# Eight softmax weight transposes on the DMA queue instead of TensorE, under a new order of the pieces

## The chip, the core and the metric

The kernel runs on one core of a Trainium2 chip. The metric is the device time of one execution in microseconds (us). Shorthand: PE is TensorE, DVE is VectorE, ACT is ScalarE, POOL is GpSimd, SP is SyncE, which here only issues transfers. SBUF is the on-chip working memory, PSUM the memory that PE writes its products to. Each engine takes its own instructions strictly in order and waits on semaphores.

## The reference

A cross attention between 512 tokens `x` and 32 state vectors `state`, for 8 batches and 8 heads of width 64, feeds a two-layer network with squared ReLU:

```python
scores  = scale * x @ state.T                    # 512 x 32
a       = softmax(scores, over the states)       # "rows"
xread   = a @ state
scores2 = scale * state @ x.T                    # 32 x 512
a2      = softmax(scores2, over the tokens)      # "columns"
sread   = a2 @ x
h = concat([xread, sread]) @ w_in                # 4352 x 512 by 512 x 2048
r = maximum(h, 0)
out = (s * r * r + b) @ w_out                    # 4352 x 2048 by 2048 x 512
```

The token rows of `xread` and the state rows of `sread` all go through the same two layers.

## The kernel before

**Pieces.** The work is cut into some 740 pieces, each a small Python function that issues a few instructions. `ORDER` (line 15) is a list of strings; the loop at line 735 walks through it and calls the pieces one after the other. A word is a name and its arguments, with the engine as a letter (A is ACT, V is DVE, G is POOL): `s.2.4.2.G` squares blocks 4 and 5 of batch 2 on POOL. There is no scheduler behind it (`manual_schedule`, line 132): the order of the words is the order on every engine and on every issuing queue. Semaphore waits between engines follow from the data and from the buffers.

**One batch b of tokens.** POOL issues the loads, which cast to 16 bits (`x`, line 182; `xn`, the same tokens in another layout, line 193). DVE transposes blocks of 32 (`xT`), PE makes the scores (`T`, line 304), DVE turns them (`U`, line 326) and takes maximum, difference (`D`, on DVE or POOL), sum and quotient (`z`, `At`) around ACT's exponential (`E1`); `A` is the row softmax. `keep` (line 320) has ACT copy the same PSUM scores to SBUF for later. PE multiplies the states into `w_in` (`M`, line 437), and ACT or DVE copies the product out (`Mc`). Then come 16 pieces `l` of layer 1 (two matmuls of 512 columns each), whose ReLU always runs on ACT (line 476), and the squares `s` on ACT, DVE or POOL (line 484). The buffers of the ReLU results turn among three, and layer 1 has two PSUM buffers. Batch 0 does a part of this in halves (`lh`, `sh`).

**Layer 2.** Batches 0 and 1 use plain products (`L`, line 512, four matmuls each). Batches 2 to 7 and the state rows use a fast 2 by 2 block multiplication with seven products (`P`, line 597, eight matmuls of 256 columns each) into PSUM tiles X, Y and W. It needs sums of blocks of the squares (`S`, line 576) and of `w_out` (`wsum`), and DVE evictions (`ev`, line 611) between products of one tile. `put` (line 619) and `out` issue the stores from SP.

**The column softmax, where the change is.** `E2` (line 388) is ACT's exponential with sums; `a2` (line 395) on DVE divides, giving 128 partitions by 1024 elements of 16 bits. `aps` (line 405) transposes this by eight PE matmuls with the identity, of 128 by 128 each, into a PSUM tile. `a2T` (line 411) copies the tile to SBUF, on ACT for seven batches and on DVE for one. `V` (line 414) is the product with `xn`, `srd` (line 434) its copy on ACT into `srdT`. All eight batches must have passed here before layer 1 of the state rows (`lsr`, line 507), near the end.

Of the kernel before, what the change touches and what calls it, by code (L numbers as in the profile page):

```python
# [11 lines left out]
FP16 = mybir.dt.float16  # L12
# [70 lines left out]
def kernel(  # L83
# [12 lines left out]
    nc = tc.nc  # L96
# [307 lines left out]

    def at_aps(b):
        at[b]["aps"] = aps = blocks(two_banks(f"aps_{b}", FP16), 0)
        for g in range(NG):
            for c in range(SCH):
                transp(aps[:, SCH * g + c], at[b]["a2"][:, g, P * c : P * c + P])

    def at_a2T(b, e):
        copy(e, sm(b, "a2T", [P, NG * SCH, P], FP16, apool, 2), at[b]["aps"])

    def at_V(*bs):

        pair = two_banks(f"vps_{bs[0]}")
# [87 lines left out]
    def square_half(b, f, p, e):  # L504
        squared(e, new_G(b, S)[:, f : f + 2, HALF * p : HALF * p + HALF], R_t.pop((b, f, p)))

    def layer1_sr(f):
        layer1("sr", f, [(w_in_f(k, f), srdT[:, k].rearrange("p n b -> p (n b)")) for k in range(NK)], B * Ns)

    ops_t = {}  # L510

    def layer2(tag, rr, q):
        if q == 0:
            ops_t[tag, rr] = ps_o.tile([P, DM], FP32, name=f"ops_{tag}_{rr}", tag="po")
        for f in range(4 * q, 4 * q + 4):
            nc.tensor.matmul(  # L516
# [252 lines left out]
```

## Time and profile before

| | |
|---|---|
| three runs | 217.42, 217.94, 218.0 us; median 217.94 |
| profiled execution | span 215.7 us from the first to the last instruction; the profile gives no other time of it, so 2.2 us of the median lie around the span |
| busy | PE 205.8 us, DVE 179.6, ACT 158.0, POOL 86.9 |
| mean granted PE clock | 0.992 |
| the eight `a2T` copies | ACT 7 of 1015 ns, DVE 1 of 681 ns |

The page gives busy time and share per engine, then the span in 40 slices of 5.4 us in which each digit is a tenth of busy time, then the DMA queues, the chain of work that ended last, and the costliest groups of instructions. A group's line gives the source line, the engine, what is written and read with its shape, the count, busy time and mean duration, and how long the engine had been idle just before such instructions and for whom. Back-to-back instructions overlap a little in the records, so mean times count is more than busy time.

### The profile page before, as it was taken

What the parts mean: (1) busy time and instruction counts of PE and PEld (TensorE: products, weight loads), DVE (VectorE), ACT (ScalarE), POOL (GpSimd) and SP (SyncE); (2) the same over time, 40 slices, a digit from 0 to 9 for tenths busy, and PEclk for the clock granted to TensorE, in tenths of its full rate; (3) what the DMA queues carried; (4) which work ended last, traced back from release to release, by engine and by line L of the source; (5) the groups of instructions that cost most, each with busy time, mean ns of one, the idle gap of its engine ahead of it and who ended that gap; (6) DMA issues with size and microseconds to landing.
All of it is one profiled execution on the core that took longest, in us unless ns stands there. A gap on an engine that the chain in (4) does not pass through costs nothing.

```text
span 215.7 us, 4829 instructions
## 1 busy us (share of the span) xinstructions
PE 205.8 (95%) x1955; PEld 130.0 (60%) x1955; DVE 179.6 (83%) x277; ACT 158.0 (73%) x260; POOL 86.9 (40%) x94
## 2 busy tenths in 40 slices
PE   7489999999999999999999999999999999999992
PEld 2134343344444448767677677677766777888881
DVE  2997899999998799969998999999986874593661
ACT  4598886899899788799999887779768475734300
POOL 8554126445093033157437057007223308916400
PEclk9969999999999999999999999999999999999999
DMA  6999998127849719523900939608902600440045
GB/s 153 175 207 206 196 206 146 41 63 106 137 106 140 133 20 171 68 50 64 162 24 2 187 112 115 82 17 145 221 8 46 144 11 0 102 97 0 5 147 145
DMA packets 23658, 22.43 MB, mean 104 GB/s; under 512 B 4436, under 2 KB 17492, under 8 KB 23636
## 3 DMA queue, kind: packets, MB, share of 16 engines
q0 software_dynamic: 16848, 12.52, 41.3%
q1 hardware_dynamic: 5504, 8.66, 14.9%
q10 hardware_dynamic: 1284, 0.95, 1.7%
q8 instruction: 15, 0.25, 0.5%
q14 instruction: 7, 0.06, 0.1%
HBM read 25.72 MB, written 8.91 MB: 161 GB/s over the span
## 4 chain that ended last, share of the span: by engine, by line
PE 91%; DMA 3%; ACT 2%; POOL 1%; DVE 1%; issue 0%; POOLq 0%
PE hps L472 25%; PE opf_X L141 20%; PE ops L516 13%; PE opf_W L141 10%; PE opf_Y L141 5%; PE mps L141 5%; DMA w_in<-in_moe_w_in_dram 3%; PE hps_sr L472 3%; PE vps L141 2%; PE aps L141 2%; PE ops_sr_X L141 2%; PE T_None L141 2%; ACT M L156 1%; PE hph L141 1%; PE ops_sr_W L141 1%; PE dps L683 1%
## 5 line engine op out<-in xcount | busy, mean ns | idle before, releaser
L476 ACT ACTIVATE r<-hps 128x512 f16<-128x512 f32 x120 | 68.8, 603 | 25.6 <-PE hps L472 22.3
L472 PE MATMUL hps<-A,M 128*128 128x512 f16 x240 | 65.6, 380 | 0.1
L141 PEld LDWEIGHTS <-g 128*128 128x128 f16 x576 | 56.0, 98 | 15.2 <-issue 0.9
L472 PEld LDWEIGHTS <-M 128*128 128x128 f16 x240 | 21.4, 98 | 19.8 <-issue 6.0
L482 POOL TENSOR_TENSOR g<-r 128x1024 f16<-128x1024 f16 (+1 forms) x9 | 21.3, 2372 | 27.0 <-ACT r L476 22.8
L156 ACT CAST M<-mps 128x1024 f16<-128x1024 f32 x29 | 29.2, 1013 | 2.3 <-PE mps L141 1.9
L516 PE MATMUL ops<-w_out,g 128*128 128x512 f16 x128 | 30.7, 379 | 0.0
L197 POOL DMA_DIRECT2D xn<-in_x_dram x32 | 18.7, 604 | 14.8 <-PE vps L141 14.0
L141 PE MATMUL opf_X<-w_T,g 128*128 128x256 f16 x192 | 24.1, 273 | 0.0
L482 DVE TENSOR_TENSOR g<-r 128x1024 f16<-128x1024 f16 (+1 forms) x30 | 22.1, 754 | 1.6 <-ACT r L476 1.6
L586 DVE TENSOR_TENSOR g<-g 128x1024 f16<-128x1024 f16 (+1 forms) x31 | 22.1, 728 | 0.2
L516 PEld LDWEIGHTS <-g 128*128 128x128 f16 x128 | 12.4, 98 | 14.9 <-POOL g L482 0.2
L615 DVE SCALAR_TENSOR_TENSOR osx<-opf_X,sb_bc,bias_bc 128x512 f32<-128x512 f32 x18 | 13.3, 740 | 7.7 <-PE opf_X L141 7.4
L357 POOL TENSOR_TENSOR At<-E,rz 128x1024 f16<-128x1024 f16 x4 | 7.7, 1914 | 21.6 <-DVE rz L348 21.6
L480 ACT ACTIVATE g<-r 128x1024 f16<-128x1024 f16 (+1 forms) x11 | 15.8, 1444 | 0.2
L141 PE MATMUL mps<-w_in,stT 64*32 64x512 f16 x256 | 13.0, 397 | 1.6 <-DMA w_in<-in_moe_w_in_dram 1.3
L586 POOL TENSOR_TENSOR g<-g 128x1024 f16<-128x1024 f16 (+1 forms) x3 | 8.3, 2768 | 15.4 <-PE opf_X L141 8.1
L141 PE MATMUL opf_W<-w_out,g 128*128 128x256 f16 x96 | 12.4, 273 | 0.0
L141 PE MATMUL opf_W<-w_T,g 128*128 128x256 f16 x96 | 12.3, 273 | 0.0
L141 PE MATMUL opf_X<-w_out,g 128*128 128x256 f16 x96 | 12.1, 273 | 0.0
L141 PE MATMUL opf_X<-w_T,S 128*128 128x256 f16 x96 | 11.8, 273 | 0.0
L141 PE MATMUL opf_Y<-w_out,g 128*128 128x256 f16 x96 | 11.8, 273 | 0.0
(102 smaller groups left out, 310.4 us busy)
## 6 DMA issues: line engine op xcount, KB each, us to landing
out_dram<-osx SPq DMA_DIRECT2D x44, 128.0 KB, 2.4
xn<-in_x_dram POOLq DMA_DIRECT2D x32, 128.0 KB, 6.7
xh<-in_x_dram POOLq DMA_DIRECT2D x14, 256.0 KB, 5.2
w_in<-in_moe_w_in_dram POOLq DMA_DIRECT2D x8, 256.0 KB, 9.2
w_out<-in_moe_w_out_dram POOLq DMA_DIRECT2D x4, 512.0 KB, 13.3
out_dram<-osb SPq DMA_DIRECT2D x16, 64.0 KB, 1.9
out_dram<-osb SPq DMA_DIRECT2D x8, 128.0 KB, 2.4
xf<-in_x_dram SPq DMA_DIRECT2D x2, 256.0 KB, 3.7
```

The costliest lines, as they stand in the source:

```text
L141: return nc.tensor.matmul(out, lhsT, rhs, start=start, stop=stop, tile_position=tp, is_transpose=is_transpose, skip_group_check=skip,)
L156: (engine.copy if engine is nc.scalar else engine.tensor_copy)(out, in_)
L197: nc.gpsimd.dma_start(out=xn_t[b][32 * jh : 32 * jh + 32].rearrange("t h c d -> t h (c d)"), in_=x[b].rearrange("h (t jh c) d -> jh t h (c ...
L357: e.tensor_tensor(out, E1, over_n(rz), ALU.mult)
L472: nc.tensor.matmul(hps, lhsT, rhs, start=(i == 0), stop=(i == len(terms) - 1))
L476: nc.scalar.activation(R_t[tag, q][:, i], hps, AF.Relu)
L480: nc.scalar.activation(g, r, AF.Square)
L482: e.tensor_mul(g, r, r)
L516: nc.tensor.matmul(ops_t[tag, rr], G_t[tag][:, f, P * rr : P * rr + P], w_out_f(f), start=(f == 0), stop=(f == NKF - 1),)
L586: e.tensor_tensor(out, x, y, op)
L615: nc.vector.scalar_tensor_tensor(out, fast(b, name[0]), s_bc, out if plus else bias, ALU.mult, ALU.add)
L683: nc.tensor.matmul(dps, ones16[:, :P], ones16, start=True, stop=True)
```

## The change

1. `aps` and `a2T` go. `tr` is one transposing DMA from SBUF to SBUF, issued by SP. It reads `a2` and writes the same tile `a2T` that the copy wrote.
2. All pieces stand in a new order.
3. Many pieces have another engine. On POOL: squares of two blocks (`s`) 7 to 15 and of four 2 to 4, halves (`sh`) 3 to 5, the state rows' (`ssr`) 0 to 2; block sums (`S`, of one half each but for one) 5 to 17 and the state rows' 2 to 4; `D` 1 to 5 and `At` 4 to 5; `wsum` 0 to 2. The copies `Mc` go from 29 on ACT and 3 on DVE to 20 and 12.
4. Accumulation begins and ends with the first and last visit to a PSUM tile, and no longer with the first and last index, so that the parts of a sum can come in any order (`L`, `P`, `cps`).

Core of the diff; of the order, its first lines and two stretches around a transpose:

```diff
-    "casts.A pair.0.4 castx.1.A idle.7 xT.0.1.0 castx.0.A xT.0.0.0 x0.1 xT.0.1.1 x0.0 idle.5 turn.0.4.A "
-    "T.0.1.0 U.0.0 win.0 win.1 keep.0.0 x.1 win.2 wout.0 xT.0.0.1 T.0.0.1 mu.0.0 D.0.V.0 win.3 keep.0.1 "
-    "U.0.1 M.1.0.1 M.0.0.0 E1.0.0 Mc.1.0.A z.0.0 mu.0.1 D.0.V.1 At.0.V.0 A.0.0 wout.1 Mc.0.0.A E1.0.1 "
...
+    "castx.1.A idle.4 x0.1 casts.A x0.0 castx.0.A win.0 xT.0.1.0 pair.0.4 turn.0.4.A idle.5 xT.0.0.0 "
+    "T.0.1.0 keep.0.0 idle.7 U.0.0 win.1 xT.0.0.1 sb xT.0.1.1 mu.0.0 x.1 T.0.0.1 keep.0.1 win.2 U.0.1 "
+    "mu.0.1 M.0.0.0 D.0.G.0 E1.0.0 Mc.0.0.A wout.0 M.1.0.1 D.0.V.1 M.1.1.0 E1.0.1 win.3 z.0.0 Mc.1.0.A "
+    "wout.1 M.0.1.1 At.0.V.0 A.0.0 lh.0.2.0 z.0.1 xT.1.0 Mc.0.1.A At.0.G.1 st Mc.1.1.A xT.1.1 lh.0.4.0 "
...
+    "keep.7 P.4.7 P.4.6 ev.4.X2 P.4.9 l.5.6 put.3.1.0 a2.0 l.5.7 D.7.G P.4.8 put.3.1.1 ev.4.W1 At.6.V "
+    "E1.7 S.4.4.0.V s.5.14.2.G l.5.4 A.6 P.4.11 ev.4.X3 l.5.2 s.5.12.2.G s.5.4.2.A nm.7 z.7 P.4.10 "
+    "nms.7.V M.6.3.1 tr.0 s.5.2.2.A",
+    "s.5.6.2.V S.5.3.1.V V.6.0 l.6.10 l.6.8 E2.7.1 s.5.0.2.G ev.4.W2 Mc.6.3.V P.4.13 S.5.3.0.G l.6.7 "
...
+    "P.6.1 ev.5.X4 S.6.2.0.G P.6.2 l.7.1 S.6.1.1.V l.7.8 E2.1.0 put.5.1.1 P.6.3 ev.6.X1 l.7.9 V.7 l.7.2 "
+    "l.7.3 P.6.4 S.6.2.1.V l.7.0 srd.7 l.7.12 s.7.8.2.G P.6.5 s.7.12.2.G S.6.4.0.V a2.1 S.6.4.1.V tr.1 "
+    "l.7.6 P.6.6 ev.6.Y s.7.0.2.A ev.6.X2 l.7.7 l.7.15 s.7.14.2.G P.6.8 V.1 s.7.2.2.V P.6.7 l.7.4 P.6.9 "
...
-    def at_aps(b):
-        at[b]["aps"] = aps = blocks(two_banks(f"aps_{b}", FP16), 0)
-        for g in range(NG):
-            for c in range(SCH):
-                transp(aps[:, SCH * g + c], at[b]["a2"][:, g, P * c : P * c + P])
-
-    def at_a2T(b, e):
-        copy(e, sm(b, "a2T", [P, NG * SCH, P], FP16, apool, 2), at[b]["aps"])
+    def at_tr(b):
+        a2T = sm(b, "a2T", [P, NG * SCH, P], FP16, apool, 2)
+        nc.sync.dma_start_transpose(out=a2T, in_=at[b]["a2"].rearrange("p g s -> p (g s)"))
...
     def layer2(tag, rr, q):
-        if q == 0:
+        v = visit("L", tag, rr)
+        if v == 1:
             ops_t[tag, rr] = ps_o.tile([P, DM], FP32, name=f"ops_{tag}_{rr}", tag="po")
...
-                start=(f == 0),
-                stop=(f == NKF - 1),
+                start=(v == 1 and f == 4 * q),
+                stop=(v == NKF // 4 and f == 4 * q + 3),
```

Batch 5's and batch 2's `V` share one piece, as do batch 6's and batch 0's; in both kernels the last `V` is that of batch 1.

More of the change, by code (lines that the diff above doesn't have):

```diff
@@ L508, in layer1_sr, with visit @@
         layer1("sr", f, [(w_in_f(k, f), srdT[:, k].rearrange("p n b -> p (n b)")) for k in range(NK)], B * Ns)
-    ops_t = {}
+    ops_t, visits = {}, {}
+    def visit(*key):
+        visits[key] = visits.get(key, 0) + 1
+        return visits[key]
     def layer2(tag, rr, q):
-        if q == 0:
+        v = visit("L", tag, rr)
+        if v == 1:
             ops_t[tag, rr] = ps_o.tile([P, DM], FP32, name=f"ops_{tag}_{rr}", tag="po")
@@ L600, in product @@
         bank, lhs, rhs = PRODUCTS[n]
-        first, last = bank not in [p[0] for p in PRODUCTS[:n]], bank not in [p[0] for p in PRODUCTS[n + 1 :]]
+        v, visits_all = visit("P", b, bank), 2 * sum(p[0] == bank for p in PRODUCTS)
         lhs = block(b, *lhs) if lhs else fast(b, "S3")
@@ L607, in product @@
                     fast(b, bank)[:, rr], lhs[:, k, P * rr : P * rr + P], w,
-                    start=(first and k == 0 and rr == 0), stop=(last and k == NKF // 2 - 1 and rr == 1), skip=True,
+                    start=(v == 1 and k == 4 * h and rr == 0),
+                    stop=(v == visits_all and k == 4 * h + 3 and rr == 1), skip=True,
                 )
@@ L660, in bias_sum @@
     def bias_sum(q):
-        if q == 0:
+        v = visit("cps")
+        if v == 1:
             cps_t.append(two_banks("cps")[:, 0, :])
@@ L667, in bias_sum @@
                 cps[32 * c : 32 * c + 32, :], ones16[:, 0:32], w_out_f(f),
-                start=(f < 4), stop=(f >= NKF - 4), tp=(0, 32 * c),
+                start=(v == 1), stop=(v == NKF // 4), tp=(0, 32 * c),
             )
@@ L728 @@
         "E1": at_E1, "z": at_z, "At": at_At, "A": at_A, "nm": at_nm, "nms": at_nms, "E2": at_E2, "a2": at_a2,
-        "aps": at_aps, "a2T": at_a2T, "V": at_V, "srd": at_srd, "M": at_M, "Mc": at_Mc,
+        "tr": at_tr, "V": at_V, "srd": at_srd, "M": at_M, "Mc": at_Mc,
         "lh": layer1_half, "sh": square_half, "l": layer1_x, "s": square, "lsr": layer1_sr,
```

111 rows, old and new, of the table ORDER are left out of this document.

## The prediction

> **What bounds the kernel now.** I first read the page's slices, then the busy time by stretches, then PE's waits. The columns of a stretch are its length, the busy time and count of PE, weight loads, DVE, ACT and POOL, the granted clock, the DMA share and GB/s.
>
> ```profile
> PE   7489999999999999999999999999999999999992
> ...
> POOL 8554126445093033157437057007223308916400
> ```
>
> ```profile
> 10.00:20.00 10.00, 8.82 (x87) 3.71 (x87) 8.70 (x18) 8.64 (x14) 4.85 (x7) 0.83 1.21 206
> 20.00:40.00 20.00, 19.64 (x151) 7.80 (x149) 19.17 (x23) 15.98 (x28) 8.57 (x8) 1.00 1.07 164
> ...
> 140.00:160.00 20.00, 20.00 (x228) 14.70 (x227) 19.19 (x31) 15.31 (x26) 6.52 (x9) 1.00 0.63 107
> 160.00:180.00 20.00, 20.00 (x198) 14.05 (x197) 14.52 (x25) 13.86 (x25) 5.51 (x3) 1.00 0.24 54
> ```
>
> From about 23 us PE has no gap until its last matmul at 211.6, at clock 1.00. PE's list of waits agrees: T, w_in and the first ReLUs, 5.7 us in all, and all before 26 us. So this kernel is a start of about 20 us, a PE stream, and a tail of 4.1 us (last eviction 0.48, last store, end). Work taken off PE's stream comes off the time one for one, as long as nothing else arrives late. The other engines matter only where they become late: DVE is at 19.2 of 20 us for long, POOL has room.
>
> The chain of waits (start, length, what) shows what PE pays for one batch's transposes, and the groups by shape show the other rows I need:
>
> ```profile
> 54.71 0.86 PE hps L472 x4
> 55.57 0.45 PE aps L141 x8
> 56.02 0.46 PE hps L472 x2
> ...
> 62.99 0.64 PE vps L141 x32
> ...
> 73.46 0.87 PE opf_X L141 x8
> ```
>
> ```profile
> L482 POOL TENSOR_TENSOR g<-r 128x1024 f16<-128x1024 f16 x7 | 13.9, 1990 | 17.0 <-ACT r L476 12.8 <-issue 4.2
> L482 POOL TENSOR_TENSOR g<-r 128x2048 f16<-128x2048 f16 x2 | 7.4, 3708 | 10.0 <-ACT r L476 10.0
> L156 ACT COPY a2T<-aps 128x1024 f16<-128x1024 f16 x7 | 7.1, 1015 | 0.0
> L141 PE MATMUL aps<-ident,a 128*128 128x128 f16 x64 | 4.9, 219 | 0.0
> ```
>
> The matmuls are 219 ns each in the records but overlap; eight hold PE for 0.45 us. From the same chain a piece `l` costs PE 0.43 us (two matmuls of the 0.86), `P` 0.87, `L` 0.86, `M` 0.3.
>
> **What is removed.** 64 matmuls: 8 x 0.45 = **3.6 us** off PE's stream. The seven copies on ACT (7.1 us) and the one on DVE (0.7) lie beside PE work; I cost them at nothing. All other pieces on PE are the same in number, so without new gaps the stream is 3.6 us shorter.
>
> **What is added: the transposing DMA.** No row of before shows one. From below it can't beat the small stores (64 KB, 1.9 us to landing); from above stand the loads of 512 KB in the crowded start, 13.3. The nearest row is the other 256 KB transfer on a hardware queue, `xf`, 3.7 us from issue to landing; I take 3.7 and keep 1.9 to 13.3. What matters is how much PE work lies between the end of `a2` and `V`. For batch 0, DVE evicts `ev.4.X2` just ahead of `a2.0`, so after `P.4.5`. Between there and `V.6.0` PE has six `P`, four `l` and one `M`: 5.25 + 1.7 + 0.3 = 7.3 us; less the eviction (0.75) and `a2` (0.86) this leaves 5.7. For batch 1, `E2.1.0` follows `l.7.8` and its ReLU; from there to `V.1` lie 8.5 us, less ReLU 0.6, exponential 0.9 and `a2` 0.86: 6.1. For batch 3 it is 9.6 - 0.86 = 8.7, for batch 2 10.9 - 0.86 = 10.0; batches 4 to 7 otherwise have over 15. With 3.7 us no `V` waits.
>
> The Trainium skill, page "VectorE: DVE Perf Modes", section "The three transpose paths", gives 1309 ns for 128 by 128 by DMA against 390 on TensorE and advises TensorE where PSUM will do; the trace's 0.45 us per eight is already far better than that 390. Eight such DMA blocks in a row would be 10.5 us (my estimate from that page). The page "DMA: Bandwidth & Descriptors", section "Latency and other measured facts", gives 261 GB/s for such transfers instead, which makes 1.0 us of data for these 256 KB (again an estimate). The two pages lie on either side of the point of decision below; no trace here shows either.
>
> **SP's queue.** `tr` waits for `a2` on SP, and stores queue behind it. The tight one is `tr.1` ahead of `put.5.1.0`, whose buffer `ev.6.W1` on DVE needs, and PE's `P.6.10` after it. Counted from `P.6.1`, `a2.1` is done near 4.5 us; two stores issue (2 x 0.6) and land (2.4) by 8.1; `P.6.7`, which the eviction waits for anyway, ends at 11.7. So 3.6 us are spare for SP's own handling of the transpose. `tr.4` stands behind the stores of `out.1.3`, but `V.4` comes 16 us of PE work later. Cost nothing.
>
> **The start.** Here the new order costs time. Before, DVE turned the first scores first, and ACT copied them after it:
>
> ```profile
> 7.13 0.72 DVE L328 STREAM_TRANSPOSE U<-T 128x512 f32<-128x512 f32 x1 [0.22 <-PE T L141]
> 7.88 0.59 ACT L324 COPY Ts<-T 128x512 f32<-128x512 f32 x1 [1.49 <-DVE U L328]
> ```
>
> ACT waited 1.49 us for DVE: two readers of this tile take turns in the order of the pieces. Now `keep.0.0` stands ahead of `U.0.0`, and `keep.0.1` ahead of `U.0.1`, so each adds its 0.59 to the chain. Seven idle matmuls (some 0.36 each, 2.5 us) and `sb` (0.4) now stand between `T.0.1.0` and `T.0.0.1` on PE. I add up: `casts` and `pair` now stand ahead of the second `xT`, so the first scores end near 7.25; plus 2.5 + 0.4 the second begin at 10.1; `T` 0.42, `keep` 0.58, then in series on DVE `U` 0.71, `mu` 0.64, `D` 0.69, `z` 0.94, `At` 0.69, `A` 0.71, with some 0.3 between: 15.8. Before, the first piece of layer 1 (`hph`) began at 13.82 by the timeline. That is +2.0, of which 0.4 is PE work already done by then; I take **+1.5** and keep +0.5 to +2.5.
>
> **The new engines.** With each piece at its row's duration, POOL goes from 88 to 155 us, DVE from 194 to 176, ACT from 176 to 163 (these sums overlap a little in truth). On average nobody is near PE's 200. POOL is, for a stretch: from `s.0.8.2.G` to the end of `s.1.12.4.G` its column holds four squares of two blocks (2.0 each), two halves (1.0), one of four blocks (3.7), two weight sums (2.15 each, by the rows of two-operand sums), `D` 2.29, `At` 1.91 and the issues of four loads (5.9): 28.1 us without a gap. That square frees the ReLU buffer that `l.2.14` needs, and PE has 29.3 us of pieces from `l.0.8` to there. The square starts about 1 us after `l.0.8`, so this is a tie, with about 1 us of slack in the two PSUM buffers. I take **+0.6** for this and its like and keep 0 to +3. In the last stage all eight parts of the block sums for the state rows are on POOL or DVE with PE work to cover them; the tail itself ends, as before, on one eviction and one store.
>
> **The sum.** -3.6 + 1.5 + 0.6 = -1.5 us against the profiled 215.7, so a span of 214.2. With the 2.2 us around the span this is **216.4** against the median of 217.94.
>
> **The rivals.**
> 1. *The start is no dearer* than one `keep` (0.6), and POOL is in time: -3.0, 214.9. For it: the PE stream was gapless before, and DVE and ACT have less to do. Against it: the chain above.
> 2. *The transpose is slow*, each of its eight blocks costing about 1 us: nothing in the trace forbids it, since even a 64 KB store needs 1.9. It decides from 5.7 us on, at `V.6.0`, then `V.1` (6.1) and `V.3` (8.7). At 8 us PE waits 2.3 + 1.9 more: 220.6, **slower than before**. At 10.5 us it would be 4.8 + 4.4 + 1.8 = 11 us more, 227.4. (That is the time by the page's 1309 ns.) Against it: the 3.7 us of `xf`, and DMA engines that the stretches above show a quarter to two thirds busy.
> 3. *POOL is late* in the stretch above: rows 10% longer, under more DVE traffic, make 28.1 into 30.9, and PE waits some 2 us there and a little later on: 218.4.
> 4. That the change does not do what it says is excluded for the 3.6 us: the matmuls are gone. They could only come back as waits.
>
> **How the numbers follow.** About 0.3% (0.65 us) is what a measurement of this kernel tells from no change. Forecast 0.42 (of it 0.32 faster, 0.08 same, 0.02 slower), first rival 0.18, second 0.24 (slower), third 0.16 (0.07 same, 0.09 slower). So faster 0.50, same 0.15, slower 0.35. The range must take in the first rival with its start at nothing (214.3) and the second at 8 us (220.6): 214.0 to 221.5 leaves out the slower half of rival two and a little below.
>
> **What would show it.** Right: no `aps` in PE's groups; the first `hph` matmul near 15.8 us; `a2T` landing about 4 us after its issue; no PE wait at `vps`; PE gapless from about 26 us. Wrong: PE waiting at `vps` for a DMA (rival two), ACT's ReLU waiting for POOL near 55 us (rival three), the first `hph` before 14.5 (rival one), or DVE evictions waiting for stores behind a transpose, which I cost at nothing.

## The result, and the profile after

The changed kernel takes **260.14 us** (median of 4 runs, 258.8 to 262.01) against 217.97 (217.42 to 218.17): a ratio of 1.194, 95% interval 1.188 to 1.200. The forecast was 216.4, the range ended at 221.5.

The slices of PE and POOL answer to those shown of before; DVE's and the granted clock belong to them:

```profile
PE   3848995799499987369976899875989899998993
...
DVE  3495798989997999998699799999899799439682
...
POOL 7367497679304689920957559493884435585620
PEclk9977999999799999959999799997999999999998
```

PE, which before had no gap from 26 us on, has holes from end to end, while DVE stands at 9 beside them. The stretches (columns as in the prediction):

```profile
10.00:20.00 10.00, 4.57 (x60) 2.00 (x59) 8.91 (x17) 5.72 (x9) 5.73 (x7) 0.81 1.21 206
20.00:40.00 20.00, 17.50 (x138) 7.61 (x137) 15.87 (x14) 15.59 (x26) 13.50 (x12) 0.92 0.91 138
100.00:120.00 20.00, 13.30 (x110) 8.11 (x109) 19.38 (x19) 8.72 (x14) 10.75 (x11) 0.83 0.83 108
140.00:160.00 20.00, 17.43 (x185) 11.25 (x185) 18.05 (x22) 12.52 (x23) 14.16 (x13) 0.91 0.43 73
160.00:180.00 20.00, 14.52 (x135) 10.17 (x135) 19.93 (x19) 9.54 (x15) 12.34 (x6) 0.92 0.38 67
```

From 100 to 120 us DVE is busy for 19.4 of 20 us with 19 instructions; before it did 31 in the same time (18.79 us). So it is not doing more, each takes longer. PE's gaps over 0.25 us, added up from its records, are 38.7 us against 4.2 before. PE's busy time is 211.9 us against 205.8 although 64 matmuls are gone: 18.4 us of it fall into five stretches in which the granted clock was 0.5 (3.4 us before), and there the matmuls of `P` start 209 ns apart, elsewhere 111. Gaps (+34.5) and busy time (+6.1) make 40.6 of the span's 41.5 us.

What PE waits for (us in total, times, longest):

```profile
PE opf_X L140 <- DVE g L585: 7.0, 3, 5.3
PE ops L515 <- DVE osb L525: 4.2, 1, 4.2
PE opf_X L140 <- DVE osx L615: 3.3, 4, 1.2
PE vps L140 <- DMA a2T<-a: 3.1, 1, 3.1
PE opf_W L140 <- DVE g L585: 3.0, 1, 3.0
PE T_None L140 <- DVE M L155: 3.0, 1, 3.0
```

DVE, in five lines of six. Its groups by shape, first of before, then of after:

```profile
L586 DVE TENSOR_TENSOR g<-g 128x1024 f16<-128x1024 f16 x30 | 20.9, 712 | 0.2
L482 DVE TENSOR_TENSOR g<-r 128x1024 f16<-128x1024 f16 x27 | 18.6, 703 | 1.6 <-ACT r L476 1.6
...
L332 DVE TENSOR_REDUCE mu<-U 128x32 f32<-128x1024 f32 x7 | 8.5, 1216 | 0.1
...
L399 DVE TENSOR_SCALAR a<-E,q 128x512 f16<-128x512 f16 x16 | 4.9, 350 | 0.3
```

```profile
L585 DVE TENSOR_TENSOR g<-g 128x1024 f16<-128x1024 f16 x21 | 30.0, 1439 | 0.2
L398 DVE TENSOR_SCALAR a<-E,q 128x512 f16<-128x512 f16 x16 | 20.6, 1325 | 0.3
...
L476 DVE TENSOR_TENSOR g<-r 128x1024 f16<-128x1024 f16 x14 | 13.9, 994 | 0.0
...
L331 DVE TENSOR_REDUCE mu<-U 128x32 f32<-128x1024 f32 x7 | 8.5, 1209 | 0.0
```

The same block sum of the same shape takes 1439 ns in place of 712, and `a2` four times its row. Reductions (1209 against 1216 before), transposes, and everything that reads PSUM kept their lengths. The timelines of DVE and POOL around 91 and 104 us show what goes on:

```profile
91.50 3.68 DVE L398 TENSOR_SCALAR a<-E,q 128x512 f16<-128x512 f16 x2
...
100.35 1.21 DVE L378 TENSOR_REDUCE nm<-Ts 128x2 f32<-128x1024 f32 x1
101.47 1.29 DVE L356 TENSOR_TENSOR At<-E,rz 128x1024 f16<-128x1024 f16 x1
...
104.07 7.24 DVE L585 TENSOR_TENSOR g<-g 128x1024 f16<-128x1024 f16 x1
```

```profile
90.78 2.13 POOL L585 TENSOR_TENSOR S<-g 128x1024 f16<-128x1024 f16 x1 [2.93 <-ACT g L474]
92.87 4.30 POOL L585 TENSOR_TENSOR g<-g 128x1024 f16<-128x1024 f16 x2
...
100.44 4.63 POOL L196 DMA_DIRECT2D xn<-in_x_dram  x8
105.07 3.62 POOL L476 TENSOR_TENSOR g<-r 128x2048 f16<-128x2048 f16 x1
108.63 2.12 POOL L585 TENSOR_TENSOR g<-g 128x1024 f16<-128x1024 f16 x1
```

One block sum that takes 0.68 us elsewhere is on DVE for 7.24: it ends at 111.31, 0.56 us after the second of two POOL instructions that it had run beside (108.63 + 2.12 = 110.75). Of the 16 divisions of `a2`, the 7 that began with nothing on POOL (once, with a copy of two elements) took 339 to 355 ns, the 8 that began beside a POOL computation 1198 to 3683, and one that began beside a load's issue and ran into a computation 2805. In the trace of before only 4 of some 120 such instructions of DVE began beside a POOL computation (518 to 1600 ns): the old order kept the two apart, and so its rows did not show this price.

To compare runs I add up what DVE's instructions last beyond the lower quartile of the same names and shape in the traces of before and after, where that is over 0.15 us, and call it **excess**: 1.5 us in 2 instructions before, 53.5 us in 31 after.

The Trainium skill, page "SBUF — State Buffer", section "Who interferes with whom", has it as a rule: a DVE instruction with two SBUF inputs contends with a GpSimd instruction that reads SBUF, one in a 2-port performance mode with GpSimd's work in general, and whichever issues first blocks the other. Most rows agree: 28 of the 31 instructions with excess began while POOL computed, and the 7 that began on an idle POOL just ahead of its next computation kept their length. Three do not fit as well. The sum of 7.24 us began 1.0 us before POOL's computation, and the division of 2805 ns 0.5 us before it, each beside the issue of a load; by their own length both should have been done by then. The third, a scaling at 35.16, began 0.13 us before. Eleven two-operand instructions that began beside such an issue were not held, so what held these stays open. I should have weighed that rule.

### The profile page after: what moved, and what is told of

Read it like the earlier page. It is cut to its first block, busy times and chain, and to the rows that moved or that the text cites. A ratio compares the mean times of both kernels' runs of the same rounds, so it can differ in the third digit from the quotient of the medians.

```text
span 257.2 us, 4724 instructions
## 1 busy us (share of the span) xinstructions
PE 211.9 (82%) x1891; PEld 129.0 (50%) x1891; DVE 215.2 (84%) x245; ACT 147.2 (57%) x249; POOL 155.6 (61%) x129
## 4 chain that ended last, share of the span: by engine, by line
PE 39%; DVE 36%; ACT 8%; issue 7%; DMA 6%; POOL 2%; ACTq 0%; DVEq 0%; POOLq 0%
PE opf_X L140 9%; PE hps L466 8%; DVE g L585 8%; PE opf_W L140 6%; DMA a2T<-a 4%; DVE osx L615 4%; ACT r L470 3%; DVE g L476 3%; DVE a L398 3%; DVE M L155 2%; PE ops L515 2%; DVE U L327 2%; PE hps_sr L466 2%; DMA ident<-ident_const 2%; PE vps L140 2%
## 5 line engine op out<-in xcount | busy, mean ns | idle before, releaser
L476 POOL TENSOR_TENSOR g<-r 128x1024 f16<-128x1024 f16 (+1 forms) x19 | 45.4, 2395 | 24.2 <-ACT r L470 24.1
L140 PE MATMUL opf_X<-w_T,g 128*128 128x256 f16 x192 | 25.4, 279 | 10.3 <-DVE g L585 7.0
L585 DVE TENSOR_TENSOR g<-g 128x1024 f16<-128x1024 f16 (+1 forms) x23 | 32.4, 1419 | 0.2
L585 POOL TENSOR_TENSOR g<-g 128x1024 f16<-128x1024 f16 x11 | 24.4, 2223 | 7.4 <-PE opf_X L140 6.3
L585 POOL TENSOR_TENSOR S<-g 128x1024 f16<-128x1024 f16 x6 | 14.4, 2409 | 19.7 <-ACT g L474 14.5
L398 DVE TENSOR_SCALAR a<-E,q 128x512 f16<-128x512 f16 x16 | 20.6, 1325 | 0.3
L155 ACT CAST M<-mps 128x1024 f16<-128x1024 f32 x20 | 20.1, 1012 | 1.0 <-PE mps L140 1.0
L476 DVE TENSOR_TENSOR g<-r 128x1024 f16<-128x1024 f16 (+1 forms) x16 | 19.9, 1245 | 0.1
L474 ACT ACTIVATE g<-r 128x1024 f16<-128x1024 f16 (+1 forms) x15 | 19.1, 1286 | 0.4 <-PE opf_X L140 0.3
L335 POOL TENSOR_TENSOR Dm<-U,mu 128x1024 f32<-128x1024 f32 (+1 forms) x5 | 9.1, 1812 | 11.6 <-DVE mu L331 11.6
L155 DVE CAST M<-mps 128x1024 f16<-128x1024 f32 x12 | 14.4, 1202 | 0.0
L356 POOL TENSOR_TENSOR At<-E,rz 128x1024 f16<-128x1024 f16 x4 | 7.9, 1968 | 10.3 <-DVE rz L347 10.3
```

The lines of the kernel that those rows point to most:

```text
L140: return nc.tensor.matmul(out, lhsT, rhs, start=start, stop=stop, tile_position=tp, is_transpose=is_transpose, skip_group_check=skip,)
L155: (engine.copy if engine is nc.scalar else engine.tensor_copy)(out, in_)
L335: e.tensor_tensor(blk(part(Dm, p)), blk(part(at[b]["U"], p)), over_n(part(at[b]["mu"], p)), ALU.subtract)
L398: nc.vector.tensor_scalar(a2[:, g].rearrange("p (c jh t) -> p jh c t", c=4, jh=4), at[b]["E2"][:, g].rearrange("p (jh c t) -> p jh c t", c ...
L474: nc.scalar.activation(g, r, AF.Square)
L476: e.tensor_mul(g, r, r)
```

## The experiments

All times are medians; before ran beside each set, at 217.8 to 218.3 us. Theory A: DVE's 16-bit work between SBUF tiles stands still while POOL computes. Theory B: the new order is late by itself. Theory C: the transposing DMA costs.

### One part of the change at a time

Both orders hold the same pieces, so order, engines and transposes can be exchanged one by one.

```diff
 f1: order and engines of before; put.2.0.1, put.3.1.0, put.3.1.1 and put.5.0.1 ahead of a tr
-aps.b ... a2T.b.A
+tr.b
 f2: order and engines of after
-tr.b
+aps.b ... a2T.b.A
 f3: order of after, tr, engines of before      f4: order of before, aps, engines of after
```

> Order and engines of before; only the 64 transposes on PE and their eight copies are replaced by the transposing DMA, at the same place of the order (three stores move ahead of a transpose on SP). Theory A (VectorE's 16-bit work between tiles in SBUF is held up while GpSimd computes; the new engines and order put the two side by side) and theory B (the new order is late by itself, whatever its engines): PE loses 3.6 us and nothing else changes, so 214.4, within 1.5. Theory C (the transposing DMA is what costs: its landing, or what it does to other DMAs): 225 or more, with PE waiting at vps.

Measured: **228.52** (ratio 1.047, 1.041 to 1.053). This is theory C's time, but not its reason: PE has no wait at `vps`. It waits for evictions instead (a section below).

> Order and engines of after, but the transposes are back on PE with their copies on ACT (one on VectorE). Theories A and B: 256 to 268, since 3.6 us of PE are added to a stream that is full of gaps. Theory C: 230 or less.

Measured: **264.3**, excess 53.4 us. The transposing DMA is not what costs the 42 us.

> Order and transposing DMA of after, but every piece on the engine that it has before (one square of four blocks goes to VectorE in place of ACT, since ACT would wait for itself). GpSimd's work falls from 155 to about 88 us. Theory A: VectorE's sums and squares go back to about 0.7 us each and the time to 216 to 232. Theory B: 245 or more, with the rows at 0.7 us. Theory C: 245 or more.

> Order and PE transposes of before, but every piece on the engine that it has after (one square on VectorE in place of ACT). GpSimd's work rises to about 155 us. Theory A: the rows of VectorE's 16-bit sums and squares grow to 1 us and more, and the time to 232 to 260. Theories B and C: 218 to 224, rows as before.

Measured: **265.2** with the old engines in the new order, **288.4** with the new engines in the old order; excess 14.0 and 35.3 us. f4 goes A's way and beyond its range. f3 goes B's way: its block sums take 858 ns, near the 712 of before, the excess falls by 39 us, and the time does not fall. Its PE waits for ACT (8.8 us for ReLUs, 7.7 for the `M` copies). My reading, which these two runs do not show, is that each order fits its own engines alone. To tell the theories apart needed cleaner runs.

### Which work of POOL holds DVE

```diff
 kernel before, 64 times between the pieces of batches 2 to 7:
+        nc.gpsimd.tensor_mul(ones16, ones16, ones16)      # g2
+        nc.gpsimd.memset(ones16, 1.0)                     # g3
+        nc.gpsimd.tensor_copy(ones16, ones16)             # i8
```

> The kernel before, with 64 multiplications added on GpSimd, each 128 by 512 in 16 bits on a tile that nobody else uses by then (about 1 us each, 64 us in all); nothing waits for them but GpSimd's own pieces behind them. Theory A (VectorE's 16-bit work between tiles in SBUF stands still while GpSimd computes): VectorE's rows of sums and squares grow by up to 1 us wherever the two meet, its busy time rises by 10 us or more, and the time to 225 or more. If the growth of these rows in the changed kernel has another cause: rows at 0.68 us as before, and a time that grows only where GpSimd's own squares come late, 218 to 222.

> The same 64 places, but each a memset of the same 128 by 512 tile on GpSimd: no operand is read. Theory A in the form that any work of GpSimd holds VectorE: as the run with multiplications, in proportion to the memsets' own length. In the form that only GpSimd's reading of operands does: VectorE's rows at 0.68 us and 218 to 222.

> The kernel before, with the 64 additions on GpSimd as copies of the 128 by 512 tile onto itself (one operand read) in place of multiplications (two read, 256.8) or memsets (none, 218.6). If any reading by GpSimd holds VectorE: 235 or more, VectorE's two-operand rows at 1 us and more. If only the second operand does: 218 to 222.

Measured: multiplications **256.8**, copies **228.0**, memsets **218.6** (ratio 1.003, 1.001 to 1.005). The groups of POOL and DVE, in the run with multiplications and in the one with memsets:

```profile
L691 POOL TENSOR_TENSOR ones<-ones 128x512 f16<-128x512 f16 x64 | 80.3, 1254 | 3.6
...
L587 DVE TENSOR_TENSOR g<-g 128x1024 f16<-128x1024 f16 x30 | 34.5, 1164 | 0.2
...
L400 DVE TENSOR_SCALAR a<-E,q 128x512 f16<-128x512 f16 x16 | 12.9, 848 | 0.3
```

```profile
L691 POOL MEMSET ones<- 128x512 f16 x64 | 33.8, 527 | 2.6
...
L587 DVE TENSOR_TENSOR g<-g 128x1024 f16<-128x1024 f16 x30 | 22.5, 766 | 0.2
...
L400 DVE TENSOR_SCALAR a<-E,q 128x512 f16<-128x512 f16 x16 | 5.8, 402 | 0.3
```

64 instructions for which no other engine waits cost 39 us. They also make POOL's own pieces late, but PE's list of waits has only 2.9 us for POOL there and over 20 for DVE: theory A by itself. DVE's excess is 45.7 us with 80.3 us of multiplications, 18.8 with 50.8 of copies, and 8.4 with 33.8 of memsets, against 1.5; beside a memset only small or one-operand work stretched: divisions, a scaling (`nms`) and a reciprocal (a division to 685 ns while a memset ran), and no two-operand sum did unless a POOL product overlapped it too. My expectation for copies (235 or more, or 222 at most) was too coarse: any operand that POOL reads holds DVE's sums, and a copy holds them for a shorter time. The rule of the Trainium skill's page "SBUF — State Buffer" given above says the same of two-operand work: it contends with reading, not with writing alone.

```diff
 g4: kernel after
     def squared(e, g, r):
+        if e is nc.gpsimd: one-element product; e.memset(g, 0.0); return
 (the same in act_sum, sum_sr and weight_sum)
```

> The changed kernel, with GpSimd's squares, block sums and weight sums left out: each is replaced by a one-element operation (so that it waits for the same things) and a memset of what it would write, so the results are not those of the reference. Order, engines, queues, transposes and every other instruction are as in the changed kernel. Theory A (the stalls of VectorE beside GpSimd are what cost): VectorE's rows near 0.7 us and 260.1 falls to 216 to 228. Theory B (the order is late by itself): 245 or more. In between if memsets hold VectorE too.

Measured: **228.4**, excess 8.2 us (53.5 in the changed kernel), just above the range of theory A (216 to 228). DVE's sums and squares are back near their rows of before:

```profile
L596 DVE TENSOR_TENSOR g<-g 128x1024 f16<-128x1024 f16 x21 | 16.1, 776 | 0.2
...
L479 DVE TENSOR_TENSOR g<-r 128x1024 f16<-128x1024 f16 x14 | 9.4, 674 | 0.0
```

So 32 of the 42 us go with POOL's squares and sums. This takes their own length along with the stalls (a memset of 1024 elements takes 0.95 us there, a sum 2.1), but PE's list of waits after holds 0.5 us for POOL; what it waited for was DVE.

```diff
 h3: kernel after
-s.*.G ssr.*.G sh.*.G   S.*.G S_sr.*.G wsum.*.G
+s.*.A ssr.*.A sh.*.A   S.*.V S_sr.*.V wsum.*.V
```

> The changed kernel with its order, its queue and its transposing DMA, but with GpSimd's squares on ACT (two on VectorE, where ACT would wait for itself) and its block sums and weight sums on VectorE: about 16 us more work on VectorE and 22 on ACT, 76 less on GpSimd. Theory A: VectorE has more to do but stands still less (55 us of excess in the changed kernel, 12 or less here), and 260.1 falls to 222 to 238. Theory B, or if GpSimd's share was needed: 245 or more.

Measured: **245.8**, excess 5.8 us (the 55 of the expectation are a coarser count of the 53.5). The stalls went as A says, but the time did not come down as far as I said and lies in theory B's range: ACT and DVE now have POOL's work. PE waits 10.3 us for ACT's ReLUs and 5.6 for DVE's sums. The same work without stalls is 14 us faster than on POOL, and still 28 us too slow for this order.

### The start

```diff
 h2: kernel before, first 57 pieces (up to A.0.1) as after    i5: g4 with the first 49 pieces of before
```

> The kernel before, with the first 57 pieces of the changed kernel, up to the first batch's A, put first in their order and on their engines; the rest as before, with PE transposes. My prediction priced this start at +1.5 (219.4). The changed kernel's first matmul of layer 1 began 3.3 us later than before (17.09 against 13.82), which makes 221.3 if it all stays. If later slack takes it up: 218.

> The run without GpSimd's squares and sums (228.4; results not those of the reference), with the first 49 pieces of the kernel before, up to the first batch's A, in their old order and on their old engines, and the rest in the order of the changed kernel. If the start costs 5.6 us here too, as it does in the order of before: 222 to 224. If slack takes it up: 227 to 229.

Measured: h2 **223.6** (ratio 1.025, 1.023 to 1.028), 5.3 us more than before; i5 **223.7**, 4.8 us less than g4. The start costs some 5 us in either order. PE in h2:

```profile
5.85 2.34 PE L681 MATMUL dps<-ones 128*128 128x512 f16 x5
8.11 0.63 PE L139 MATMUL T<-xT,stZ 64*32 64x256 f16 x16
8.67 1.69 PE L681 MATMUL dps<-ones 128*128 128x512 f16 x7
...
10.91 0.42 PE L139 MATMUL T<-xT,stZ 64*32 64x256 f16 x16 [0.25 <-ACT sb_bc L654]
...
16.59 1.01 PE L139 MATMUL hph<-A,M 128*128 128x256 f16 x4 [0.17 <-DVE A L370]
19.20 1.03 PE L139 MATMUL hph<-A,M 128*128 128x256 f16 x4 [1.59 <-ACT M L154]
```

Five idle matmuls (`dps`) stand ahead of the first `T` and seven behind it, so the first scores begin at 8.11, not 6.64; and the second pair of `hph` waits for ACT's copies of `M`.

### The transposing DMA in the order of before

In f1 SP shows what happened at the last transpose; the chain of waits goes through the stores behind it:

```profile
180.51 1.26 SPq L414 DMA_TRANSPOSE a2T<-a  x1
181.82 2.52 SPq L626 DMA_DIRECT2D out_dram<-osx  x4
```

```profile
PE opf_W L139 <- DVE osx L617: 5.3, 2, 4.9
PE opf_X L139 <- DVE osx L617: 2.3, 1, 2.3
```

SP stood at the transpose, waiting for `a2`, with stores of finished results behind it; the next eviction needed their buffer, and PE the eviction.

```diff
 g1: f1 with every store ahead of tr.b whose evictions stand ahead of a2.b
-tr.1 ... put.5.1.0 ... put.5.1.1
+put.5.1.0 put.5.1.1 tr.1
 h4: order and stores of before, the transpose issued by ACT at the place of the copy
-        nc.sync.dma_start_transpose(...)
+        nc.scalar.dma_start_transpose(...)
 h1: g1 with s.5.2.2, s.5.6.2, s.5.14.2, s.6.2.2 on ACT in place of DVE
```

> The first run (transposing DMA alone in the order and on the engines of before, 228.5) with one thing changed: on SP every store whose evictions come ahead of a batch's a2 now also stands ahead of that batch's transpose, so that no store waits for the softmax. If what cost 10.7 us there is that SP waits in order at the transpose and holds stores, and with them the output buffers (theory D): 214 to 216, PE gapless, no eviction waiting for a store. If it is the transposing transfer itself that slows stores and loads beside it (theory C): 224 or more, with landings of the stores near 5 us as there.

Measured: **219.44** (ratio 1.005, 1.002 to 1.008). This lies between the two forecasts: SP's order was 9 of the 10.7 us, but PE's 3.6 us do not show as gain.

> Order, engines and stores of before; the transposing DMA stands in place of the copy after the PE transposes, and ACT issues it (1.25 us of ACT in place of the copy's 1.0), so that SP's stores never wait for the softmax. If SP's order was the cost of the first run (228.5): 215 to 218, PE waiting at vps at most where under 4 us of PE work stand between issue and V. If the transfers beside the stores cost: 219 to 224.

Measured: **223.2** (1.023, 1.021 to 1.026). The transfers land in 2.8 us at the median, and no `V` waits for one. Two other waits cost. One is for stores again, beside loads (one issued at 122.87 took 7.1 us; this run alone does not show that the loads slowed it). The other is in the chain of that run:

```profile
106.46 5.03 DMA a2T<-a
...
111.59 0.61 DVE a L397 x2
```

`a2` has one buffer. The next batch's `a2` on DVE may not overwrite it until the transfer has read it, and DVE's evictions stand behind. PE's matmuls used to read `a2` in 0.45 us.

> The run with sorted stores (219.4; transposing DMA alone in the order of before), and four squares of batches 5 and 6 moved from VectorE (0.69 us each) to ACT (1.05 each), which has the room that the seven copies left. There the 3.6 us that PE lost came back as gaps, most of them between 120 and 160 us, where VectorE is busy 19 of 20 us. If VectorE is what bounds that stretch: 2.8 us less of it there, and 216 to 217.5. If the stores' landing is what binds there: no change, 218.5 to 220.

Measured: **218.97** (1.006, 1.001 to 1.011). DVE's load does not bind there; a gap of 1.6 us near 150 us stayed.

```diff
 i4: g1
-xn.0 xn.7 ... xn.1
+xn.0 ... xn.7 xn.1
 i7: g1, with both loads behind a copy of two elements on POOL that reads ev.5.X1's result
-xn.7 ... xn.1
+ev.5.X1 after xn.7 xn.1
```

> The run with the transposing DMA alone and sorted stores (219.4), with one load moved: batch 7's second copy of x is loaded about eleven microseconds of PE work later, so that it does not run beside the stores of batch 4, whose landing (5.9 us against 2.4 in the kernel before) held an eviction and PE for 1.8 us near 150 us. If the loads slow those stores: that gap goes, 216 to 217.8. If the transposing transfer does: 218.5 to 220.

Measured: **218.56** (1.000, 0.997 to 1.004). It tested nothing: POOL has no work between the two places, and the load started with the end of `vps` as before. Hence i7.

> The run with the transposing DMA alone and sorted stores (219.4), with the two loads of x that follow batches 6 and 0's read (8 transfers, 1 MB) held back by a copy of two elements on GpSimd that waits for the first eviction of batch 5. If these loads are what makes the stores of batch 4 land late (5 to 6 us against 2.4): the gap of 1.8 us near 150 us goes, and with it 216 to 217.5, faster than before. If the transposing transfer does: 218.5 to 220, gap unchanged.

Measured: **216.43** (ratio 0.993, 0.991 to 0.995): 0.7% faster than before, and the fastest of all. POOL's loads, the eviction, and the stores issued from 142 to 149 us (their number, size and median time to landing), in g1 and then in i7:

```profile
145.07 3.42 POOL L194 DMA_DIRECT2D xn<-in_x_dram  x6 [12.40 <-PE vps L138]
...
150.96 0.75 DVE L616 SCALAR_TENSOR_TENSOR osx<-opf_X,sb_bc,bias_bc 128x512 f32<-128x512 f32 x1 [2.59 <-DMA out_dram<-osx]
...
out_dram<-osx SPq DMA_DIRECT2D x8, 128.0 KB, 5.9
```

```profile
150.59 3.55 POOL L195 DMA_DIRECT2D xn<-in_x_dram  x6 [0.15 <-PE opf_Y L139]
...
149.05 0.75 DVE L617 SCALAR_TENSOR_TENSOR osx<-opf_X,sb_bc,bias_bc 128x512 f32<-128x512 f32 x1 [0.27 <-DMA out_dram<-osx]
...
out_dram<-osx SPq DMA_DIRECT2D x7, 128.0 KB, 2.4
```

With PE ahead by a microsecond, `V` released the buffer of `xn` earlier in g1 (`vps` began at 144.06, in the kernel before at 145.27), and the loads ran into batch 4's stores: 5.9 us to landing against 2.4. With the loads held back, the stores land in 2.4 again and the gap is gone. That the loads slow these stores is shown. Why they did so less in the kernel before, where they began 2.3 us after the first of these stores and not 1.9, was not tested. The trace of g1 is from one of its faster executions (218.17 us), so the two traces account for 1.6 of the 3.0 us between the medians. PE's last matmul ends at 210.65 against 211.62: of the 3.6 us, 1.0 is kept. Most of the rest is in the records of i7. The 240 matmuls of layer 1 take 1.5 us more (232 ns apart, not 226), and 1.4 of it is five steps of 341 to 692 ns among steps of 216; two of these are waits for ACT's ReLU (0.31 and 0.25 us), the other three stay open. The idle matmuls of the start take 0.8 us more; over the first 20 us the granted clock was 0.83 and not 0.91.

### What else there is in the changed kernel

```diff
 i1: g4 with aps and a2T as in f2
 i6: i1 with the start of i5, and D and At on POOL replaced as the squares are
```

> The run without GpSimd's squares and sums (228.4; results not those of the reference), with the transposes back on PE and their copies on ACT (one on VectorE) as in the second run. If the transposing DMA is part of the 10 us that are left: 222 to 227. If it pays even here: 230 to 233, by the 3.6 us of PE.

> The same with the transposes on PE too, and GpSimd's remaining products (Dm and At) also replaced by one-element operations and memsets (results not those of the reference): GpSimd then does no two-operand work of size, the start and the transposes are those of before, and what is left of the change is the order of the pieces after the start and the engines of VectorE's and ACT's pieces. If the order by itself is sound: 217 to 221. If theory B holds for part of the loss: 224 or more.

Measured: i1 **230.4**, so that in the new order the transposing DMA gains 2.0 us (two runs on each side, 229.5 to 231.4 and 226.9 to 229.9: its size is uncertain); i6 **225.1**, 7 us above before, as theory B has it for a part of the loss. From 40 us on, PE has seven gaps of 0.3 to 0.9 us there, 3.3 in all, for ReLUs and copies of `M` and `a2T` that stand late on ACT, and DVE still has 2.9 us of excess. That part of the order's cost is spread and was not divided further.

So the 42 us are, as far as it is settled: 32 with POOL's squares and sums, 5 from the start, some 7 from the order and the engines besides, and 2 gained by the transposing DMA.

## Why the prediction was wrong, step by step

1. **What bounds the kernel now** was read rightly, but "the other engines matter only where they become late" took their rows as given. DVE was at 19 of 20 us, so a stretching of its instructions had little room before it reached PE.
2. **The new engines: "With each piece at its row's duration, POOL goes from 88 to 155 us, DVE from 194 to 176" is the step that failed.** POOL's figure came true (its rows now add up to 158.8); DVE's rows add up to 228.3, not 176, and the 52 us between are the excess. The rows of before held for a DVE that POOL hardly met. The +0.6 (0 to 3) that I took for POOL was a search for late POOL pieces, and the only PE wait for POOL was 0.5 us; the price was on the other engine, 53.5 us of excess, worth 32 us of time (g4). No rival named it. Rival three had POOL's rows "10% longer, under more DVE traffic", the mirror image and far too small.
3. **The start: +1.5 (0.5 to 2.5)** was the right sign and too small: some 5 us (h2, i5). The chain that I added up put the first scores' end near 7.25; they ended at 9.02 (8.39 + 0.63), since I did not count the five idle matmuls ahead of them. The first `hph` came at 17.09, not 15.8, and the next pair 2.6 us later behind `M`'s copies, which I had not looked at.
4. **The transposing DMA: 3.7 us to landing** was good: 2.7 at the least, 2.8 at the median. Two took far longer, both among loads of POOL: 9.8, issued at 101.68, for which the trace shows no wait of PE, and 10.9, issued at 131.61 between loads of `xn` and `xh` that were in flight. PE waited 3.1 us for the latter, where batch 2's cover was to be 10.0. The 10.5 us for eight blocks, my estimate from the Trainium skill's page "VectorE: DVE Perf Modes", section "The three transpose paths", was not borne out: the measured 2.8 decides.
5. **SP's queue: "Cost nothing"** held in the changed kernel, where evictions did not wait for stores, but only by its order: in the order of before the same step costs 9 us (f1 against g1). What I did not see at all is that a transfer reads `a2` for longer than PE did and holds its only buffer (h4).
6. **What is removed: 3.6 us** left PE's stream. In the order of before it was paid back in waits until a load was moved (g1 219.4, i7 216.4); there it is worth 0.7%.
7. **Rival two** had the sign, and its mechanism only in the 3.1 us of point 4.

## What to carry to other kernels

A row of the profile holds for the company it kept: before a piece is moved onto GpSimd, look what VectorE does at that time. In these runs, work of VectorE with two SBUF operands, and scalings of one, mostly stood still when it began while GpSimd computed on operands that it read (a sum went from 712 to 1164 ns at the mean beside 64 multiplications, a division from 350 to 848). Reductions (1209 ns against 1216), VectorE's transposes (1232 against 1235) and work that reads PSUM kept their lengths. A transfer that takes the place of a matmul and a copy adds three things to check: what its queue holds back while it waits, how long its source buffer stays taken, and which transfers now start earlier and land beside others.

## What the hardware showed that I had not expected

- One DVE instruction can lose to POOL twice in a row: a sum of 0.68 us ended 6.6 us late, after two POOL instructions back to back (3.62 and 2.12 us), although it began 1.0 us before the first. POOL is held too: its 64 multiplications took 1254 ns at the mean, 1040 where no two-operand instruction or scaling of DVE met them.
- A transposing DMA of 128 by 1024 elements of 16 bits keeps its issuing queue for 1.25 us. It lands 2.7 us after issue at the least; the median was 2.8 us in the changed kernel and 5.1 in g1, and two, beside loads, took 9.8 and 10.9.
- Stores of 128 KB that land in 2.4 us took 5 to 7 us beside loads issued by POOL.
